# Attention and a top-2 mixture of experts in one kernel: the first expert's weights are split later and on VectorE, its early units start after one matrix, and they take two steps a tile

## The chip, the cores and the metric

The kernel runs on one core of one Trainium2 chip. The metric is device time in microseconds (us) of one execution; less is better. The runs of the kernel before took 970.3, 971.06 and 975.12 us, median 971.06. A separate execution, with the profiler, took 977.14 us; its span from the first to the last instruction is 975.3 us, and 1.8 us lie around it.

## The reference

```python
kv = np.einsum('bhsd,bhse->bhde', k, v)            # 8 batches, 8 heads, 576 rows, 64 wide
out = np.einsum('bhsd,bhde->bhse', q, kv)
rms = np.sqrt(np.mean(out * out, axis=-1, keepdims=True) + 1e-06)
x = (out / rms * g_norm)                           # as 4608 rows (tokens) of 512
...
noisy_logits = x @ w_gate + np.log1p(np.exp(x @ w_noise)) * noise
top2 = np.argpartition(-noisy_logits, 2, axis=1)[:, :2]     # 2 of 8 experts a token
...                                                # top2_w: softmax over the two
for e in range(E):
    for k in range(2):
        mask = top2[:, k] == e
        h = np.maximum(x[mask] @ w1[e], 0.0)       # 512 -> 1024
        out[mask] += top2_w[mask, k, None] * (h @ w2[e])    # 1024 -> 512
```

All inputs and the output are float32.

## The kernel before

The engines are called PE (matmul), PEld (its weight loads), DVE (VectorE), ACT (ScalarE), POOL (GpSimd) and SP (which issues DMAs). Each engine runs its own queue in order; the order of the code is the order of every queue.

**Attention.** The 4608 tokens are 36 tiles of 128. A tile's matmuls (`tile_mm`, L590) multiply q with a prepared k'v of its batch; four of the tiles lie across two batches, so there are 40 pieces. `prep` (L551 to L581) makes the next batch's k'v in steps between the pieces: PE matmuls L558, L568 and L577, with ACT copies L563, L571 and L580 between them. `advance` takes finished tiles on: ACT copies a tile out of the two PSUM buffers "big" (L598) and squares it (L605), DVE sums the squares (L607), ACT makes the root (L611, L612), POOL scales (L621, L625), DVE adds up the logits (L630), ACT issues the store of x to DRAM (L634). After a piece PE gets KW = 8 small matmuls of zeros (`keep_warm`, L124) while the tile number is under KT = 24; they compute nothing that is used.

**Gating.** After tiles 10, 18, 28 and 36 a chunk of tokens is gated (`chunk`, `gating`): the two experts of each token, the place of each token in its expert's list (`onehots` L304 to L310, `place` L318) and the gate's weight. `finish` (L325) turns expert 0's list, as far as it is known, into row numbers and gates, and `scale_gates` multiplies the gates with a constant "c" that is known when both of the expert's matrices have been scaled. These steps are generators; `pump` takes them on, several times a tile.

**Experts.** Float32 is split into two float16 halves, and three matmuls take the place of one. `weights` (L214) loads w1 and w2 of an expert (`load_w1` L206, `load_w2` L212, on SP), finds the largest value of each (L221 on DVE, four times), gets it to all partitions through PE (L232), and splits the matrix. For experts 1 to 7 ACT writes the high half with the scale (L255) and DVE the low half (L257). For expert 0 ACT scales in place (L250), copies the high half (L251), and POOL subtracts (L248). Expert 0's steps are taken on twice a tile from tile W1 = 2.

Work on an expert goes in units of token tiles. A unit gathers its rows of x (`gather`, L360), transposes them (`xpose`, L385 on PE for the first units), does the first layer (`l1`, L434, out through ACT L439 and DVE L440) and the second (`l2`, L478, out through ACT L503), and scatters its results (`scatter`, L412). The units are numbered from 0; expert 0 has units 0 to 4. Units 0 to 2 (EARLY) of two tiles each begin while attention still runs: `moe_early` waits until "c" is known and all of expert 0's weights are in, then puts the unit's `l1` and `l2` into `early`, and `fill_early`, once after each tile, takes one step: 12 matmuls of L434 or 6 of L478. Expert 1 begins with unit 5. After attention `bg` holds the next experts' background steps: `locate` makes an expert's list (L318 into M), `prepare` its weights.

Before the first scatter the output must be zero: `clear` (L402) issues 18 DMAs of 512 KB from a row of zeros. Here ACT issues them, one beside each early step once attention is over (`held`).

All DMAs of SP and ACT share eight semaphores, given out in turn, so a DMA waits for the one that had its semaphore before, and what stands behind it on its engine waits as well.

Of the kernel before, what the change touches and what calls it, by code (L numbers as in the profile page):

```python
# [14 lines left out]
AF = mybir.ActivationFunctionType  # L15
# [16 lines left out]
CHUNKS = (10, 18, 28, 36)  # L32
SL, W1 = 2, 2
KT, KV2 = 24, 0
XW, PY = 2, 6
LAG = 2
KC, KR, KQ, KX, KO = 5, 1, 4, 3, 3
GY = 3
WY = 4
YG, YX = 5, 2  # L40
KW0, KW1, KW = 100, 10, 8
# [10 lines left out]
def attention_moe(ctx: ExitStack, tc: tile.TileContext, kvm, kvr, qt, gn, wgn, noise, w1, w2, out):  # L52
# [160 lines left out]

    def weights(e, pool, lo, slack=0):  # L214
        WT[e] = w = {}
# [27 lines left out]

        def split(src, hi, lw, s):
            if lo is G:
                for c in range(5):
                    if c:
                        G.tensor_tensor(lw[:, c - 1], src[:, c - 1], hi[:, c - 1], OP.subtract)  # L248
                    if c < 4:
                        A.activation(src[:, c], src[:, c], AF.Copy, scale=s)  # L250
                        A.activation(hi[:, c], src[:, c], AF.Copy)  # L251
                    yield
                return
            for c in range(4):
                A.activation(hi[:, c], src[:, c], AF.Copy, scale=s)  # L255
                if c:
                    lo.scalar_tensor_tensor(lw[:, c - 1], src[:, c - 1], s, hi[:, c - 1], op0=OP.mult, op1=OP.subtract)  # L257
                yield
            lo.scalar_tensor_tensor(lw[:, 3], src[:, 3], s, hi[:, 3], op0=OP.mult, op1=OP.subtract)
            yield  # L260
            yield
# [9 lines left out]
        w["w1l"] = pool.tile([P, 4, FF], F16, name="w1l")  # L271
        yield from split(r1, w["w1h"], w["w1l"], sc[:, 1:2])
        for _ in range(min(slack, 3)):
            yield
        if (e, 1) not in RW:
# [12 lines left out]
        w["w2l"] = pool.tile([P, 4, FF], F16, name="w2l")  # L288
        yield from split(r2, w["w2h"], w["w2l"], sc[:, 4:5])
        for k in ("w2h", "w2l"):  # L290
# [108 lines left out]
    def clear():  # L399
        r = next(blank, None)  # L400
        if r is not None:
            zeroed.append(A.dma_start(ov[:, r:r + 2], zrow[:, None, :].to_broadcast([P, 2, DM])).ins)  # L402
            return True
# [66 lines left out]
    def l2(u):  # L470
# [18 lines left out]
        for i, t in enumerate(tiles):  # L489
            if tail:  # L490
                ps = pss[i]
            else:
                ps = ps_tile([P, DM])
                for f in range(0, 8, 2):
                    mms(ps, i, (f, f + 1))
                    if f < 6:
                        yield
            if len(outs) == 4:
                while clear():
                    pass  # L500
                scatter()
            y = moe_a.tile([P, DM], F32, name="y", bufs=4)
            A.activation(y, ps, AF.Copy, scale=LG[e][:, t:t + 1])  # L503
            outs.append((y, e, t))
            if u >= EARLY:
                scatter()
            yield
# [6 lines left out]
    def moe_early(u):  # L514
        while "c" not in WT[0]:
            yield 1
        finish(0, M0, slice(2 * u, 2 * u + 2))
        yield 1
        gather(u)
        yield YG  # L520
        while 0 not in loaded:
            yield 1
        yield from xpose(u)
        early.extend([l1(u), l2(u)])

    early = deque()
    held = [0]
    ready, loaded = {0}, set()

    with tc.tile_pool(name="p1", bufs=2) as p1, tc.tile_pool(name="ps1", bufs=1, space=PSUM) as ps1:  # L530
# [148 lines left out]
        def fill_early():  # L679
            while early:  # L680
                try:
                    next(early[0])
                    if held[0] and not clear() and held[0] > 1:
                        scatter()
# [4 lines left out]
        def first_weights():  # L689
            yield from weights(0, wts_a, G, SL)  # L690
            loaded.add(0)
# [12 lines left out]
        for b in range(B):  # L704
# [4 lines left out]
            if b + 1 < B:  # L709
                load_q(b + 1, 1)  # L710
            if b + 2 == B:
                load_w1(1)
            steps = prep(b + 1) if b + 1 < B else iter(())
            for args in per[b]:
                t = args[0]
                tile_mm(*args)
                keep_warm(KW if t < KT else KV2)
                next(steps, None)
# [14 lines left out]
            drain(steps)  # L733
        held[0] = 1
        for t in range(NT, NT + 4):
# [19 lines left out]
    def prepare(e):  # L755
        yield from weights(e, wts_b if e % 2 else wts_a, V)
        if e in ready:
# [6 lines left out]
    def locate(e):  # L764
        M = psl.tile([P, 5 * CAP], F32, name="M")
        last = None
        for q in range(5):
            oh = (yield from onehots(e, 9 * q, 9 * q + 9)) if q < 4 else None
            if q:
# [10 lines left out]
    def fill():  # L780
        hold[0] -= 1
        if bg and hold[0] <= 0:
            try:
                hold[0] = next(bg[0]) or 1
            except StopIteration:
                bg.popleft()

    bg.append(prepare(1))
    k = 0
    while side:  # L790
        pump()
        fill_early()
        k += 1
        if k % 2:
            fill()
    finish(0, M0, slice(2 * EARLY, CAP))
    gather(EARLY)
    held[0] = 2
    tot = rout.tile([P, E], F32, name="tot")
# [12 lines left out]
    V.tensor_scalar(over[:, 0:1].bitcast(I32), over[:, 1:2], float(CAP * P), None, op0=OP.is_gt)  # L812
    bg.appendleft(locate(1))
    if GB > 4:
# [13 lines left out]
    for u in range(EARLY, len(units) + 1):  # L828
        if u < len(units):
# [10 lines left out]
            if u > EARLY:  # L840
                while clear():
                    pass
                scatter()
# [103 lines left out]
```

## Time and profile before

| | |
|---|---|
| runs | 970.3, 971.06, 975.12 us |
| profiled execution | 977.14 us, span 975.3 us, mean granted clock 0.965 |
| PE busy | 916.5 us (94% of the span) |
| DVE, ACT, POOL busy | 445.7, 327.5, 387.5 us |
| moved by DMA | 143.33 MB, mean 147 GB/s |
| filler L124 | 406 matmuls, 32.9 us |

Matmuls are pipelined and their modelled ends overlap, so PE's work is best read from starts. Idle time is listed with what ended it; the idle time of an engine matters only where another one waits for it.

### The profile page before, as it was taken

The numbers are of one execution on the slowest core, as the hardware profiler recorded it, in microseconds if no ns is written. First come the engines' busy times: TensorE is split into PE (matmuls) and PEld (weight loads), VectorE is DVE, ScalarE is ACT, GpSimd is POOL, SyncE is SP. The second block draws the span as 40 slices with busy tenths as digits, with TensorE's granted clock in tenths as the row PEclk, the third lists the DMA queues.
The fourth block names the chain that finished last, engine by engine and source line by source line (L and its number), as shares of the span: only waits on it lengthen the run. The fifth ranks groups of instructions, "written<-read, shape, count | busy, mean of one in ns | idle before, by whom it ended". The sixth has DMA issues, their size and how long they took to land. (4 is left out here: it accounts for less than half of the span.)

```text
span 975.3 us, 15946 instructions
## 1 busy us (share of the span) xinstructions
PE 916.5 (94%) x6484; PEld 517.2 (53%) x6484; DVE 445.7 (46%) x936; ACT 327.5 (34%) x519; POOL 387.5 (40%) x412
## 2 busy tenths in 40 slices
PE   9976888988999999999999999999998989999995
PEld 8866775657444644464445444554443434644452
DVE  1648658554745543545353444455264447311110
ACT  1576543222522341233224332333243223332111
POOL 0456645153523542344245234414342544242122
PEclk9978799988999999999999999999999999999998
DMA  8999655952963864485357544666349735362224
GB/s 329 364 348 350 207 195 198 385 98 57 254 116 76 169 169 60 97 171 135 84 102 132 152 116 92 142 104 164 66 120 127 187 76 92 50 113 45 44 37 58
DMA packets 123534, 143.33 MB, mean 147 GB/s; under 512 B 79632, under 2 KB 79760, under 8 KB 123408
## 3 DMA queue, kind: packets, MB, share of 16 engines
q1 hardware_dynamic: 95696, 80.68, 30.2%
q0 software_dynamic: 17920, 41.95, 23.2%
q10 hardware_dynamic: 9792, 18.88, 5.1%
q8 instruction: 97, 1.59, 0.7%
q14 instruction: 29, 0.24, 0.1%
HBM read 83.02 MB, written 40.11 MB: 126 GB/s over the span
## 5 line engine op out<-in xcount | busy, mean ns | idle before, releaser
L434 PE MATMUL pp<-xT,w1h 128*128 128x512 f16 (+5 forms) x1600 | 367.8, 327 | 5.9 <-DVE oa L304 2.6
L478 PE MATMUL pp<-w2h,hT 128*128 128x512 f16 x1200 | 365.6, 381 | 5.4 <-ACT hT L439 4.1
L478 PEld LDWEIGHTS <-hT 128*128 128x128 f16 x1800 | 175.9, 98 | 214.0 <-issue 9.3
L412 POOL DMA_INDIRECT out_rows<-y,row x80 | 129.9, 1624 | 359.2 <-ACT y L503 354.5
L440 DVE SCALAR_TENSOR_TENSOR hT<-pp,hT 128x512 f16<-128x512 f32 x160 | 108.0, 688 | 353.7 <-ACT hT L439 353.6
L434 PE MATMUL pp<-xT,w1l 128*128 128x512 f16 (+5 forms) x800 | 256.8, 327 | 0.0
L478 PE MATMUL pp<-w2l,hT 128*128 128x512 f16 x600 | 228.2, 380 | 0.0
L434 PEld LDWEIGHTS <-w1h 128*128 128x128 f16 x1600 | 151.2, 100 | 112.2 <-issue 8.0
L439 ACT ACTIVATE hT<-pp 128x512 f16<-128x512 f32 x160 | 92.5, 596 | 265.7 <-PE pp L434 255.1
L503 ACT ACTIVATE y<-pp,gate 128x512 f32<-128x512 f32 x80 | 54.0, 686 | 258.6 <-PE pp L478 201.5
L360 POOL DMA_INDIRECT xg<-xs,idx x80 | 85.0, 1063 | 91.7 <-DVE la L332 43.5
L434 PEld LDWEIGHTS <-w1l 128*128 128x128 f16 x800 | 79.8, 100 | 56.5 <-issue 1.8
L368 POOL TENSOR_TENSOR xh<-xg,xh 128x512 f16<-128x512 f32 x70 | 91.4, 1380 | 35.7 <-ACT xh L367 35.6
L221 DVE TENSOR_REDUCE mx<-rw 128x1 f32<-128x1024 f32 x64 | 74.7, 1208 | 1.3 <-DMA rw<-w 1.3
L367 ACT ACTIVATE xh<-xg 128x512 f16<-128x512 f32 x70 | 41.1, 624 | 22.7 <-DMA xg<-xs,idx 18.8
L590 PE MATMUL big<-kvw,qt 64*128 64x80 f32 (+1 forms) x640 | 45.5, 287 | 2.2 <-ACT kvw L580 2.1
L304 DVE TENSOR_TENSOR oa<-jb,lnb 128x1152 bf16<-128x1152 bf16 (+2 forms) x32 | 46.3, 1448 | 0.0
L590 PEld LDWEIGHTS big<-kvw,qt 64*128 64x128 f32 (+1 forms) x640 | 39.1, 189 | 8.2 <-ACT kvw L580 2.8
L607 DVE TENSOR_REDUCE ss<-sq 128x16 f32<-128x1024 f32 x18 | 21.9, 1215 | 47.2 <-ACT sq L605 47.1
L411 POOL MEMSET tick<- 1x1 f32 x80 | 38.7, 484 | 0.0
L625 POOL TENSOR_TENSOR x<-o,ss 128x512 f32<-128x512 f32 x36 | 38.0, 1076 | 0.0
L257 DVE SCALAR_TENSOR_TENSOR w1l<-rw,sc,w1h 128x1024 f16<-128x1024 f32 x21 | 27.3, 1333 | 22.3 <-ACT w1h L255 22.3
(140 smaller groups left out, 587.7 us busy)
## 6 DMA issues: line engine op xcount, KB each, us to landing
rw<-w SPq DMA_DIRECT2D x64, 512.0 KB, 7.2
kvc<-kvm SPq DMA_DIRECT2D x32, 512.0 KB, 8.0
xs<-x ACTq DMA_DIRECT2D x18, 512.0 KB, 5.9
out_rows<-zrow ACTq DMA_DIRECT2D x18, 512.0 KB, 7.5
qt<-qt SPq DMA_DIRECT2D x8, 640.0 KB, 8.3
qt<-qt SPq DMA_DIRECT2D x8, 512.0 KB, 7.9
kvr<-kvr SPq DMA_DIRECT2D x4, 512.0 KB, 6.9
xg<-xs,idx POOLq DMA_INDIRECT x80, 3.9
```

The lines of the kernel that those rows point to most:

```text
L221: V.tensor_reduce(mx[:, c:c + 1], src[:, c], axis=AX.X, op=OP.max, apply_absolute_value=True)
L304: V.tensor_tensor(oa, jb[:, None, :].to_broadcast([P, n, P]), lnb[:, s, e:e + 1].to_broadcast([P, n, P]), OP.is_equal)
L360: G.indirect_dma_start(out=x, out_offset=None, in_=src, in_offset=bass.IndirectOffsetOnAxis(ap=LI[e][:, t:t + 1], axis=0))
L367: A.activation(x[:, 0], XG[u, t], AF.Copy)
L368: G.tensor_tensor(x[:, 1], XG[u, t], x[:, 0], OP.subtract)
L412: d = G.indirect_dma_start(out=out, out_offset=bass.IndirectOffsetOnAxis(ap=LS[e][:, t:t + 1], axis=0), in_=y, in_offset=None, compute_op= ...
L434: T.matmul(ps[:, f % ps.shape[1], 0:n], w[wn][:, c, f * P:(f + 1) * P], x[:, xo + c, 0:n], start=(c == 0 and k == 0), stop=(c == HP - 1 an ...
L439: A.activation(h[:, 0, f:f + nf, 0:n], ps, AF.Relu)
L440: V.scalar_tensor_tensor(h[:, 1, f:f + nf, 0:n], ps, 0.0, h[:, 0, f:f + nf, 0:n], op0=OP.max, op1=OP.subtract)
L478: T.matmul(ps, h[:, hk, f, i * P:(i + 1) * P], w[wn][:, f], start=(f == 0 and k == 0), stop=(f == 7 and k == 2))
L503: A.activation(y, ps, AF.Copy, scale=LG[e][:, t:t + 1])
L590: T.matmul(TL[t][r0:r0 + n, h, hp * 80:(hp + 1) * 80], q[r, hp, s0 - o:s0 - o + n], KVW[b][r, hp], start=True, stop=True, skip_group_check ...
```

## The change

- W1 goes from 2 to 7: expert 0's weights start five tiles later. KT goes from 24 to 16: no filler from tile 16 on.
- Expert 0's split is done as the other experts': one ACT instruction and one DVE instruction a quarter, and with `slack` one more step between them.
- A flag "half" is set when w1 is split. `moe_early` now finishes the list and gathers without waiting for "c"; gates that lack "c" are kept in `bare` and multiplied when the weights are done. Transposes and `l1` wait for "half" alone; `second` lets `l2` wait for all weights. YG, the steps between gather and transposes, goes from 5 to 7.
- `fill_early` is called twice a tile.
- The 18 zeroing DMAs go to SP's queue, all at the start of batch 6 (tile 27), ahead of expert 1's w1.
- After attention expert 1's `locate` comes before its `prepare` and begins while the last chunk is still being gated (its last quarter waits for that); a background step is taken at every turn instead of every other, and scatters begin after the last list is finished. XW, the steps ahead of the transposes of units 3 and 4, goes from 2 to 5.

```diff
-SL, W1 = 2, 2
-KT, KV2 = 24, 0
-XW, PY = 2, 6
+SL, W1 = 2, 7
+KT, KV2 = 16, 0
+XW, PY = 5, 6
...
-YG, YX = 5, 2
+YG, YX = 7, 2
...
-        def split(src, hi, lw, s):
-            if lo is G:
-                for c in range(5):
-                    if c:
-                        G.tensor_tensor(lw[:, c - 1], src[:, c - 1], hi[:, c - 1], OP.subtract)
-                    if c < 4:
-                        A.activation(src[:, c], src[:, c], AF.Copy, scale=s)
-                        A.activation(hi[:, c], src[:, c], AF.Copy)
-                    yield
-                return
+        def split(src, hi, lw, s, slack=0):
             for c in range(4):
                 A.activation(hi[:, c], src[:, c], AF.Copy, scale=s)
+                if slack:
+                    yield
                 if c:
-                    lo.scalar_tensor_tensor(lw[:, c - 1], src[:, c - 1], s, hi[:, c - 1], op0=OP.mult, op1=OP.subtract)
+                    V.scalar_tensor_tensor(lw[:, c - 1], src[:, c - 1], s, hi[:, c - 1], op0=OP.mult, op1=OP.subtract)
                 yield
...
-        yield from split(r1, w["w1h"], w["w1l"], sc[:, 1:2])
-        for _ in range(min(slack, 3)):
-            yield
+        yield from split(r1, w["w1h"], w["w1l"], sc[:, 1:2], slack)
+        w["half"] = True
...
-            zeroed.append(A.dma_start(ov[:, r:r + 2], zrow[:, None, :].to_broadcast([P, 2, DM])).ins)
+            zeroed.append(SP.dma_start(ov[:, r:r + 2], zrow[:, None, :].to_broadcast([P, 2, DM])).ins)
...
     def moe_early(u):
-        while "c" not in WT[0]:
-            yield 1
         finish(0, M0, slice(2 * u, 2 * u + 2))
+        if "c" not in WT.get(0, ()):
+            bare.append(slice(2 * u, 2 * u + 2))
         yield 1
         gather(u)
         yield YG
-        while 0 not in loaded:
+        while "half" not in WT.get(0, ()):
             yield 1
         yield from xpose(u)
-        early.extend([l1(u), l2(u)])
+        early.extend([l1(u), second(u)])
+
+    def second(u):
+        while 0 not in loaded:
+            yield
+        yield from l2(u)
...
+            while bare:
+                scale_gates(0, bare.pop())
             loaded.add(0)
...
             if b + 2 == B:
+                while clear():
+                    pass
                 load_w1(1)
...
                 tile_mm(*args)
+                fill_early()
                 keep_warm(KW if t < KT else KV2)
...
-        held[0] = 1
...
         for q in range(5):
+            while q == 3 and side:
+                yield 1
...
+    bg.append(locate(1))
     bg.append(prepare(1))
-    k = 0
     while side:
         pump()
         fill_early()
-        k += 1
-        if k % 2:
-            fill()
+        fill()
     finish(0, M0, slice(2 * EARLY, CAP))
     gather(EARLY)
-    held[0] = 2
+    held[0] = 1
...
-    bg.appendleft(locate(1))
```

Three places of the order show what moves. The first is ACT's queue at the split of expert 0's w1. Before, around tile 11 (`o` and `sq` are attention's copy and square, `kvw` is the k'v copy L563, `ss` the root):

```order
L605 ACTIVATE sq<-o 128x1024
L250 ACTIVATE rw<-rw,sc 128x1024
L251 ACTIVATE w1h<-rw 128x1024
L250 ACTIVATE rw<-rw,sc 128x1024
L251 ACTIVATE w1h<-rw 128x1024
L563 ACTIVATE kvw<-kvt 128x4x64
L611 ACTIVATE ss<-ss,eps 128x16
L612 ACTIVATE ss<-ss 128x16
L598 ACTIVATE o<-big 128x640
```

And now, around tile 15:

```order
L601 ACTIVATE sq<-o 128x1024
L246 ACTIVATE w1h<-rw,sc 128x1024
L559 ACTIVATE kvw<-kvt 128x4x64
L154 ACTIVATE gt_d<-gt_d 128x10
L607 ACTIVATE ss<-ss,eps 128x16
L608 ACTIVATE ss<-ss 128x16
L594 ACTIVATE o<-big 128x640
L246 ACTIVATE w1h<-rw,sc 128x1024
```

Four split instructions stood ahead of the k'v copy; now it is one, and the next comes after the next tile's copy.

The second is SP's queue from the loads of the last batches' k, v and q (`kvc`, `qt`) on. Before:

```order
L536 DMA kvc<-kvm 128x1024 x4
L548 DMA qt<-qt 128x1280 x2
L548 DMA qt<-qt 128x1024
L206 DMA rw<-w 128x1024 x4
L212 DMA rw<-w 128x2x512 x4
```

And now; the second matrix of expert 0 (`rw`, first row) has moved here, from ahead of batch 5's k and v to ahead of batch 7's:

```order
L212 DMA rw<-w 128x2x512 x4
L544 DMA qt<-qt 128x1024
L532 DMA kvc<-kvm 128x1024 x4
L544 DMA qt<-qt 128x1280 x2
L544 DMA qt<-qt 128x1024
L394 DMA out_rows<-zrow 128x2x512 x18
L206 DMA rw<-w 128x1024 x4
```

The zeroing stands between the last load of q and expert 1's w1.

The third is DVE's queue after attention, where the last chunk's lists are made (`oa`, `ob` of 128x1024 and 128x400 belong to the last chunk of expert 0, those of 128x1152 and 128x450 to `locate` of expert 1). Before, nothing of `locate` stands there, and the weights of expert 1 are being scaled (`sc`):

```order
L196 CAST vals<-gt_w 128x64
L304 TENSOR_TENSOR oa<-jb,lnb 128x1024
L307 TENSOR_TENSOR ot<-tb_101,t_115 128x80
L310 TENSOR_TENSOR ob<-ot,vals 128x400
L234 TENSOR_REDUCE al<-pp 128x1
L235 TENSOR_SCALAR al<-al 128x1
```

And now:

```order
L302 TENSOR_TENSOR ob<-ot,vals 128x450
L196 CAST vals<-gt_w 128x64
L381 TENSOR_TENSOR xT<-pp,xT 128x4x128
L296 TENSOR_TENSOR oa<-jb,lnb 128x1024
L299 TENSOR_TENSOR ot<-tb_101,t_115 128x80
L302 TENSOR_TENSOR ob<-ot,vals 128x400
L296 TENSOR_TENSOR oa<-jb,lnb 128x1152
```

Two quarters of expert 1's lists are now made before the last chunk's, between its steps, the other two follow at once, and expert 1's weights come after.

On PE the first matmul of unit 0's first layer stands after tile 25 (before: after tile 24); each tile then has two early steps instead of one, and when the last tile's matmuls are issued unit 0 is done and 24 matmuls of unit 1 stand before them, where before unit 0 had 30 of its 48 second-layer matmuls left. From the first matmul of expert 1 on, PE's order is the same.

More of the change, by code (lines that the diff above doesn't have):

```diff
@@ L212, in load_w2, with weights @@
             SP.dma_start(r[:, c].rearrange("p (f d) -> p f d", f=2), v[c])
-    def weights(e, pool, lo, slack=0):
+    def weights(e, pool, slack=0):
         WT[e] = w = {}
@@ L242, in scale @@
             yield
-        def split(src, hi, lw, s):
-            if lo is G:
-                for c in range(5):
-                    if c:
-                        G.tensor_tensor(lw[:, c - 1], src[:, c - 1], hi[:, c - 1], OP.subtract)
-                    if c < 4:
-                        A.activation(src[:, c], src[:, c], AF.Copy, scale=s)
-                        A.activation(hi[:, c], src[:, c], AF.Copy)
-                    yield
-                return
+        def split(src, hi, lw, s, slack=0):
             for c in range(4):
                 A.activation(hi[:, c], src[:, c], AF.Copy, scale=s)
+                if slack:
+                    yield
                 if c:
-                    lo.scalar_tensor_tensor(lw[:, c - 1], src[:, c - 1], s, hi[:, c - 1], op0=OP.mult, op1=OP.subtract)
+                    V.scalar_tensor_tensor(lw[:, c - 1], src[:, c - 1], s, hi[:, c - 1], op0=OP.mult, op1=OP.subtract)
                 yield
-            lo.scalar_tensor_tensor(lw[:, 3], src[:, 3], s, hi[:, 3], op0=OP.mult, op1=OP.subtract)
+            V.scalar_tensor_tensor(lw[:, 3], src[:, 3], s, hi[:, 3], op0=OP.mult, op1=OP.subtract)
             yield
@@ L288, in weights @@
         w["w2l"] = pool.tile([P, 4, FF], F16, name="w2l")
-        yield from split(r2, w["w2h"], w["w2l"], sc[:, 4:5])
+        yield from split(r2, w["w2h"], w["w2l"], sc[:, 4:5], slack)
         for k in ("w2h", "w2l"):
@@ L498, in l2 @@
             if len(outs) == 4:
-                while clear():
-                    pass
                 scatter()
@@ L520, in moe_early @@
         yield YG
-        while 0 not in loaded:
+        while "half" not in WT.get(0, ()):
             yield 1
         yield from xpose(u)
-        early.extend([l1(u), l2(u)])
+        early.extend([l1(u), second(u)])
[3 more added lines that the diff above has]
+        yield from l2(u)
     early = deque()
+    bare = []
     held = [0]
@@ L682, in fill_early @@
                     next(early[0])
-                    if held[0] and not clear() and held[0] > 1:
+                    if held[0]:
                         scatter()
@@ L689, in first_weights @@
         def first_weights():
-            yield from weights(0, wts_a, G, SL)
+            yield from weights(0, wts_a, SL)
+            while bare:
+                scale_gates(0, bare.pop())
             loaded.add(0)
@@ L755, in prepare @@
     def prepare(e):
-        yield from weights(e, wts_b if e % 2 else wts_a, V)
+        yield from weights(e, wts_b if e % 2 else wts_a)
         if e in ready:
@@ L840, in attention_moe @@
             if u > EARLY:
-                while clear():
-                    pass
                 scatter()
```

## The prediction

> **What bounds the kernel now.** I cut the span at the starts of attention tiles 0, 14 and 24, at the end of the last attention tile's matmuls, and at the first matmul of expert 1, and asked for busy time in these windows. The columns are the window, its length, then busy us (instructions) of PE, PEld, DVE, ACT and POOL, the granted clock, the DMA share and GB/s.
>
> ```profile
> core 0: us, PE busy (x) PEld busy (x) DVE busy (x) ACT busy (x) POOL busy (x), PEclk, DMA share, GB/s
> 0.00:19.20 19.20, 17.44 (x293) 16.51 (x293) 2.57 (x16) 2.48 (x4) 1.00 (x8) 1.00 0.86 325
> 19.20:70.20 51.00, 43.52 (x769) 38.02 (x768) 24.73 (x46) 30.97 (x52) 24.88 (x24) 0.87 0.94 351
> 70.20:113.20 43.00, 33.10 (x508) 29.01 (x506) 29.91 (x132) 25.29 (x45) 28.68 (x33) 0.80 0.80 295
> 113.20:154.30 41.10, 36.52 (x471) 29.13 (x469) 27.21 (x104) 21.67 (x44) 18.51 (x25) 0.96 0.52 180
> 154.30:254.60 100.30, 87.70 (x656) 60.79 (x655) 59.37 (x159) 27.32 (x45) 38.81 (x47) 0.91 0.67 199
> 254.60:960.00 705.40, 694.83 (x3788) 342.40 (x3786) 301.88 (x481) 218.46 (x328) 271.73 (x273) 1.00 0.54 111
> ```
>
> From 254.6 us on PE is busy for 694.83 of 705.40 us at full clock, and the change leaves that order of instructions as it is: this part is carried over unchanged. All that can move lies before. I call the four windows from 19.2 to 254.6 **first** (tiles 0 to 13), **second** (tiles 14 to 23), **third** (tiles 24 to 35, with early expert work between them) and **bridge** (the rest of expert 0). In none of them is PE full: 7.5, 9.9, 4.6 and 12.6 us are idle, and the clock is under 1.
>
> Next I asked who PE waited for, first from 50 to 113 us, then in the bridge. The columns are the waiting and the awaited instruction, us in total, times, longest.
>
> ```profile
> PE kvt L568 <- ACT kvw L563: 5.9, 2, 3.9
> PE kvt L577 <- ACT kvT L571: 4.7, 2, 3.4
> PE big L590 <- ACT kvw L580: 2.1, 2, 1.6
> ```
>
> ```profile
> PE pp L385 <- DMA xg<-xs,idx: 5.9, 2, 3.6
> PE M L318 <- DVE ob L310: 3.3, 1, 3.3
> PE pp L232 <- DVE dg L228: 1.6, 1, 1.6
> PE RM L318 <- DVE ob L310: 1.5, 1, 1.5
> ```
>
> So 12.7 us of the 17.4 us idle in the first two windows are waits for ACT in the k'v preparation of the next batch. ACT's timeline shows why ACT was late: it was in the split of expert 0's first matrix.
>
> ```profile
> 52.18 1.06 ACT L251 ACTIVATE w1h<-rw 128x1024 f16<-128x1024 f32 x1
> 53.14 1.13 ACT L250 ACTIVATE rw<-rw,sc 128x1024 f32<-128x1024 f32 x1
> 54.30 1.06 ACT L251 ACTIVATE w1h<-rw 128x1024 f16<-128x1024 f32 x1
> 55.27 0.36 ACT L563 ACTIVATE kvw<-kvt 128x256 f32<-128x256 f32 x1
> ```
>
> The reader sees two pairs back to back, and L563, for which PE stands still, behind them. PE's timeline at the same place shows the second cost, a slow clock after the gap (start, length, line, idle in brackets):
>
> ```profile
> 55.69 1.06 PE L568 MATMUL kvt<-ident,kvw 128*64 128x128 f32 x4 [3.94 <-ACT kvw L563]
> 56.72 2.00 PE L590 MATMUL big<-kvw,qt 64*128 64x80 f32 x16
> ...
> 71.75 1.12 PE L590 MATMUL big<-kvw,qt 64*128 64x80 f32 x16
> 72.81 0.62 PE L124 MATMUL RM<-zrow 128*128 128x128 f16 x8
> ```
>
> The same 16 matmuls of a tile take 2.00 us at 56.72 and 1.12 at 71.75.
>
> **The split (first and second window).** These are the groups of the split before, and the DVE instruction that the other experts use for the low half, which expert 0 now uses too:
>
> ```profile
> L250 ACT ACTIVATE rw<-rw,sc 128x1024 f32<-128x1024 f32 x8 | 9.1, 1138 | 4.1 <-DVE sc L241 2.2 <-DVE sc L238 1.9
> L251 ACT ACTIVATE w1h<-rw 128x1024 f16<-128x1024 f32 x4 | 4.2, 1056 | 0.1
> L251 ACT ACTIVATE w2h<-rw 128x1024 f16<-128x1024 f32 x4 | 4.2, 1057 | 0.1
> L248 POOL TENSOR_TENSOR w1l<-rw,w1h 128x1024 f16<-128x1024 f32 x4 | 8.5, 2128 | 4.3 <-ACT w1h L251 4.3
> L257 DVE SCALAR_TENSOR_TENSOR w1l<-rw,sc,w1h 128x1024 f16<-128x1024 f32 x21 | 27.3, 1333 | 22.3 <-ACT w1h L255 22.3
> ```
>
> ACT loses eight 1.06 us passes (8.4 us). POOL loses twice 8.5 us and was not waited for by PE, so that is worth nothing by itself. DVE gains 8 x 1.333 = 10.7 us, half in the second window, half in the third. The order puts one split instruction of ACT between attention's, two pieces of the old block never together, so the 3.9 us wait and its twin for the second matrix lose their cause; what is late next is DVE's chain or a load.
>
> First window: 7.5 us idle at most, and nothing at least, because the load of w1 now starts at tile 7, behind the loads of the next batch on SP's queue, at 351 GB/s, and DVE's first reduction of it can wait there, with the sums of squares queued behind it and ACT waiting for those. I take 5 us, about the block from 52 us on and the slow clock after it.
>
> Second window: DVE was busy 29.91 us and gets 4 x 1.333 = 5.3 more, so it can't be under 35.2 us; the data, 295 GB/s x 43.0 us = 12.7 MB, at the first window's 351 GB/s needs 36.1. The gain is thus at most 6.9 us. Nine of the filler groups (0.62 us each, 5.6 us) go as well, but they lie inside that bound and are no term of their own. DVE may also wait for w2, whose load now stands behind batch 6's on SP. At least it is nothing; I take 5.
>
> **The third window and the two steps a tile.** Early unit 0 starts its first layer after tile 25 (before: 24), but does it two steps a tile, and its second layer too. By the last tile 30 more matmuls of L478 and 24 more of L434 are issued. Their price, from PE's rows: 18 of L478 from 185.21 to 189.09 (0.216 each) and 24 of L434 to 191.71 (0.109):
>
> ```profile
> 185.21 0.38 PE L478 MATMUL pp<-w2h,hT 128*128 128x512 f16 x1
> ...
> 189.09 0.38 PE L434 MATMUL pp<-xT,w1h 128*128 128x256 f16 x2
> ...
> 191.71 0.37 PE L318 MATMUL RM<-ob,oa 128*128 128x50 bf16 x8
> ```
>
> That is 6.5 + 2.6 = 9.1 us, paid in the third window and saved in the bridge: it moves work and gains nothing by itself. It would gain where it filled an idle PE, at most the 4.6 us idle there; but DVE goes from 27.21 to 32.5 us with w2's low half, and w2's ACT passes now stand here, so it may also lose as much. I take nought.
>
> **The zeroing.** Eighteen DMAs of 512 KB move from ACT's queue after the last tile to SP's, ahead of w1 of expert 1, at the start of batch 6. In the bridge they held ACT up:
>
> ```profile
> 169.86 7.59 ACTq L402 DMA_DIRECT2D out_rows<-zrow  x2
> 177.50 0.60 ACT L439 ACTIVATE hT<-pp 128x512 f16<-128x512 f32 x1 [7.07 <-DMA rw<-w]
> ```
>
> Now they are 18 x 0.524 = 9.4 MB, 27 us at 351 GB/s, in a window that used 180 GB/s of it. What is queued behind them on SP is w1 of expert 1, before at 121.70, first needed now after unit 3 has begun, late in the bridge: hidden.
>
> ```profile
> 121.70 2.42 SPq L206 DMA_DIRECT2D rw<-w  x4
> ```
>
> **The bridge.** Lists of expert 1 (L318 M) now come before its weights, and the pieces that PE waited 3.3 us for stand between early steps. Between the placing of the last tokens and unit 3's transposes PE has 24 + 36 early matmuls, 2.6 + 7.8 = 10.4 us, where before it reached them early and waited 3.6 us for the rows; unit 2's 2.3 us go likewise. That is 9.2 us at most. Against it: with 9.1 us less early work to hide the last tokens' gating, and unit 2's results now waiting behind the first scatters, some of the waits come back; the 1.6 us for L228 stays. At least nothing; I take 5.
>
> **Sum.** 5 + 5 + 0 + 5 = 15 us. The profiled execution took 977.1 us (span 975.3, 1.8 around it), so it would take 962.1. It lies 6.1 us above the median of the runs, 971.06, and 15 off the median gives **956**. With the ends together: 7.5 + 6.9 + 9.2 = 23.6 gives 947; 2 + 2 + 1 = 5, what I would still call this case, gives 966.
>
> **Rivals.** A measurement of this kernel tells a change from none at about 0.5%, 4.9 us.
>
> *The front is held anyway* (0.17). DMA is at 0.94 in the first window, and DVE stands near its floor in the second; if loads and DVE replace ACT as the wait, tile 24 starts at 113 again and only the bridge gains: 971 - 0 to 5, so 966 to 971. For it: DVE's 5.3 us more. Against it: the waits on record name ACT.
>
> *The clock falls without filler* (0.11). From tile 16 on PE has real work for half a tile's time. The matmuls after the 3.94 us gap ran at 2.00 for 1.12, and a gap of 1.47 was enough too:
>
> ```profile
> 77.48 0.64 PE L577 MATMUL kvt<-gw,kvT 64*64 64x16 f32 x16
> ...
> 135.87 0.63 PE L385 MATMUL pp<-ident,xg 128*128 128x128 f32 x4 [1.47 <-DVE ss L613]
> 136.43 1.01 PE L577 MATMUL kvt<-gw,kvT 64*64 64x16 f32 x16
> ```
>
> (L577: 1.01 for 0.64.) Nine groups without filler at 0.88 us more are 7.9 us: 956 + 8 = 964. [...]
>
> *Slower: zeroing chokes the third window* (0.10). The eight hardware DMA semaphores are taken in turn, and ACT's stores of x wait for zeroing DMAs that had the semaphore before, as L439 did for 7.07 us; unit 1's gather runs in the same stretch, and PE, in order, stands at its transposes before the next tile:
>
> ```profile
> 130.25 0.99 POOL L360 DMA_INDIRECT xg<-xs,idx  x1 [4.11 <-DVE la L332]
> ```
>
> Transposes followed that gather after 5.6 us (135.87). With three such waits, 3 x 7.07 = 21 us, less the 10 us of the first two windows: 982. It decides from the point where a zeroing DMA lands later than three tiles after its issue (3 x 41.1 / 12 = 10 us); before, they landed in 7.5:
>
> ```profile
> out_rows<-zrow ACTq DMA_DIRECT2D x18, 512.0 KB, 7.5
> ```
>
> *All of it comes* (0.10): the bounds above and some of the third window's idle, 944 to 947.
>
> **How the numbers follow.** The forecast has 0.52. Faster by over 0.5%: 0.52, the last rival's 0.10, 0.08 of the clock's 0.11 and 0.05 of the held front's 0.17, together 0.75. Within 0.5%: 0.12 of the held front and 0.03 of the clock, 0.15. Slower: 0.10. The range reaches from 944 to 973: it takes in the forecast's 947 to 966, the held front and the clock, and leaves out the slower case and the extreme of the best.
>
> **What would show it.** Right: no wait of over 2 us of PE for L563's and L571's counterparts; tile 24 at about 103 us; the last tile ending at 150 to 156 in spite of 9 us more work in it; expert 1's first matmul at about 240. Wrong: tile 24 still at 113 with PE or ACT waiting for DVE or a load; ACT's stores of x waiting for out_rows between tiles 28 and 35; the second window's clock under 0.80; or waits of 10 us and more in the bridge, so that what the front gains is given back.

## The result, and the profile after

The changed kernel took 960.98 us (median of 10 runs, 955.41 to 964.66), the kernel before in the same sitting 971.94 us (965.55 to 977.01): ratio 0.9896, 95% interval 0.9871 to 0.992. That is faster by 11.0 us, 1.0%; 956 had been forecast, with 944 to 973 as range. The profiled execution took 961.43 us, 15.7 less than that of before.

Cut at the same five places (tile 0, tile 14, tile 24, the end of the last tile's matmuls, expert 1's first matmul), the changed kernel's windows read:

```profile
core 0: us, PE busy (x) PEld busy (x) DVE busy (x) ACT busy (x) POOL busy (x), PEclk, DMA share, GB/s
0.00:19.36 19.36, 17.60 (x291) 16.67 (x292) 2.57 (x16) 2.48 (x4) 1.00 (x8) 1.00 0.85 326
19.36:63.84 44.48, 41.17 (x769) 36.37 (x767) 20.36 (x46) 22.95 (x44) 16.39 (x20) 0.92 0.95 360
63.84:100.19 36.35, 27.13 (x435) 24.04 (x431) 34.21 (x129) 20.38 (x40) 18.51 (x24) 0.81 1.02 378
100.19:152.28 52.09, 46.83 (x528) 34.59 (x527) 35.88 (x125) 28.27 (x52) 25.11 (x35) 0.97 0.92 339
152.28:240.78 88.50, 76.38 (x600) 52.68 (x600) 57.13 (x150) 24.46 (x42) 35.11 (x42) 0.92 0.49 119
240.78:959.60 718.82, 696.89 (x3803) 343.57 (x3801) 301.29 (x481) 219.97 (x331) 275.38 (x277) 0.99 0.54 110
```

Against before: first window 51.0 to 44.5 us, second 43.0 to 36.4, third 41.1 to 52.1, bridge 100.3 to 88.5, the rest 720.7 to 718.8. In the second window DVE is now busy for 34.21 of 36.35 us and the DMA share is 1.02: DVE has taken ACT's place, and no wait of PE or DVE there names a load. PE's waits there (the columns are as before: us in total, times, longest):

```profile
PE big L586 <- ACT kvw L576: 3.5, 2, 2.8
PE RM L310 <- DVE ob L302: 3.3, 1, 3.3
PE kvt L573 <- ACT kvT L567: 1.7, 1, 1.7
```

No wait is left for the copy that was L563 (now L559), and for L571's counterpart L567 at most 1.7 us; before, the longest were 3.9 and 3.4. A new wait for DVE, at the lists, has come. The longest for L580's counterpart L576 has grown from 1.6 to 2.8 us; just before that copy ACT itself had waited 2.30 us for DVE, in the gating (at 89.47 us).

In the bridge there is a new wait as well. This is the longest row of PE's waits in the bridge:

```profile
PE pp L426 <- ACT xT L380: 6.1, 2, 5.1
```

ACT's timeline shows what its transposed rows (L380) stood behind:

```profile
189.43 0.60 ACT L431 ACTIVATE hT<-pp 128x512 f16<-128x512 f32 x1 [2.23 <-PE pp L426]
203.43 0.69 ACT L493 ACTIVATE y<-pp,gate 128x512 f32<-128x512 f32 x1 [13.40 <-DMA out_rows<-y,row]
204.01 0.59 ACT L380 ACTIVATE xT<-pp 128x512 f16<-128x512 f32 x1
205.81 0.69 ACT L493 ACTIVATE y<-pp,gate 128x512 f32<-128x512 f32 x1 [1.21 <-DMA out_rows<-y,row]
```

There are four buffers for results (`y`). The fifth waits 13.4 us until the first scatter has read one out; the first scatter is issued at 198.51, behind unit 3's gathers, though the fourth result had been ready at 172.3:

```profile
193.44 0.99 POOL L352 DMA_INDIRECT xg<-xs,idx  x1 [17.96 <-DVE m L327]
198.51 1.62 POOL L404 DMA_INDIRECT out_rows<-y,row  x1 [0.22 <-issue]
```

### The profile page after: what moved, and what is told of

It is laid out like the page before. It is cut to its first block, busy times and chain, and to the rows that moved or that the text cites. A ratio compares the mean times of both kernels' runs of the same rounds, so it can differ in the third digit from the quotient of the medians.

```text
span 959.6 us, 15796 instructions
## 1 busy us (share of the span) xinstructions
PE 906.0 (94%) x6412; PEld 507.9 (53%) x6412; DVE 451.4 (47%) x944; ACT 318.5 (33%) x511; POOL 371.5 (39%) x404
## 5 line engine op out<-in xcount | busy, mean ns | idle before, releaser
L426 PE MATMUL pp<-xT,w1h 128*128 128x512 f16 (+5 forms) x1600 | 366.6, 326 | 14.1 <-ACT xT L380 6.1
L470 PE MATMUL pp<-w2h,hT 128*128 128x512 f16 x1200 | 365.1, 380 | 4.2 <-ACT hT L431 4.2
L470 PEld LDWEIGHTS <-hT 128*128 128x128 f16 x1800 | 175.2, 98 | 210.9 <-issue 4.7
L426 PE MATMUL pp<-xT,w1l 128*128 128x512 f16 (+5 forms) x800 | 255.4, 326 | 0.0
L470 PE MATMUL pp<-w2l,hT 128*128 128x512 f16 x600 | 227.6, 379 | 0.0
L426 PEld LDWEIGHTS <-w1h 128*128 128x128 f16 x1600 | 149.8, 99 | 119.2 <-issue 9.6
L426 PEld LDWEIGHTS <-w1l 128*128 128x128 f16 x800 | 79.1, 99 | 58.4 <-issue 3.7
L586 PE MATMUL big<-kvw,qt 64*128 64x80 f32 (+1 forms) x640 | 46.4, 289 | 3.7 <-ACT kvw L576 3.7
L586 PEld LDWEIGHTS big<-kvw,qt 64*128 64x128 f32 (+1 forms) x640 | 39.8, 192 | 10.5 <-ACT kvw L576 4.6
L250 DVE SCALAR_TENSOR_TENSOR w1l<-rw,sc,w1h 128x1024 f16<-128x1024 f32 x24 | 31.1, 1327 | 23.5 <-ACT w1h L246 23.5
L621 POOL TENSOR_TENSOR x<-o,ss 128x512 f32<-128x512 f32 x36 | 40.0, 1132 | 0.0
```

The source lines that it names most:

```text
L426: T.matmul(ps[:, f % ps.shape[1], 0:n], w[wn][:, c, f * P:(f + 1) * P], x[:, xo + c, 0:n], start=(c == 0 and k == 0), stop=(c == HP - 1 an ...
L470: T.matmul(ps, h[:, hk, f, i * P:(i + 1) * P], w[wn][:, f], start=(f == 0 and k == 0), stop=(f == 7 and k == 2))
L586: T.matmul(TL[t][r0:r0 + n, h, hp * 80:(hp + 1) * 80], q[r, hp, s0 - o:s0 - o + n], KVW[b][r, hp], start=True, stop=True, skip_group_check ...
```

## The experiments

The **theory** after this reading: the split's form and its later start free the front; the second step only moves work; the zeroing, in the third window, loads the DMA engines; the bridge gains by the early lists and loses by the queue behind the first scatters. The **rivals** are in the expectations. Each kernel has one edit to the changed kernel where nothing else is said; times are medians, ratios are to the kernel before on the same chip (its medians 970.71 to 971.75). Line numbers are those of the changed kernel (L951 and L952 are the old split's two passes; L586 is a tile's matmuls, L426 and L470 are the two layers, L377 the transposes, L380 and L381 their copies, L310 the matmuls of the lists and L302 what DVE makes for them). The same instructions in the same order took 42.9 to 45.7 us in the first window and 718.0 to 721.2 in the last part, so a difference of under 3 us in one window tells nothing by itself. In the bridge the changed kernel's order took 85.4 us in one of the runs below (the filler until tile 23) and 88.5 in its own; in the third window the order with one step took 48.3 and 43.4.

**Scatters allowed from the end of attention on.**

```diff
-            drain(steps)
+            drain(steps); held[0] = int(b == B - 1)
```

> The changed kernel with one edit: results of the early units may be scattered from the end of attention on, not only after the last gather of unit 3. In the changed kernel PE waited 5.05 us at 207.04 us for ACT's transposed rows, which stood behind a result (y) that waited 13.4 us for the first scatters to free its buffer. Theory (the new wait is that queue on ACT, and the change put it there): four scatters now run in the 18 us in which POOL had nothing to do, ACT's wait shrinks below 2 us, and 3 to 5 us go: 956 to 958. Rival (PE would wait for the gathered rows or for DVE anyway): the wait changes its name and less than 1.5 us goes: 959.5 to 961.

It took 952.94 us, ratio 0.9814 (0.9783 to 0.9846), 8.0 less than the changed kernel. POOL's timeline, and the bridge:

```profile
151.13 1.63 POOL L404 DMA_INDIRECT out_rows<-y,row  x1 [0.16 <-issue]
...
168.49 1.57 POOL L404 DMA_INDIRECT out_rows<-y,row  x1 [0.40 <-ACT xT L380]
```

```profile
147.90:230.34 82.44, 73.19 (x600) 51.96 (x601) 58.12 (x150) 25.02 (x42) 36.72 (x43) 0.98 0.52 126
```

Four scatters now run before 170 us, ACT's wait of 13.4 us is gone, PE's for L380 is 1.1 us in place of 6.1, and the bridge is 82.4 us long in place of 88.5. The wait was the queue on ACT, and the theory holds. Its price is less sure than the 8.0: 4.4 of the 8.8 us between the two profiled executions lie ahead of tile 35's end, where the edit changes nothing, and in the bridge PE's idle time falls by 2.9 us, from 12.1 to 9.2.

**The old split, at the new place.** Expert 0's quarters go through two ACT passes and POOL, two quarters to a tile, as before.

```diff
-        yield from split(r1, w["w1h"], w["w1l"], sc[:, 1:2], slack)
+        yield from split(r1, w["w1h"], w["w1l"], sc[:, 1:2], slack) if e else old_split(nc, r1, w["w1h"], w["w1l"], sc[:, 1:2])
...
-        yield from split(r2, w["w2h"], w["w2l"], sc[:, 4:5], slack)
+        yield from split(r2, w["w2h"], w["w2l"], sc[:, 4:5], slack) if e else old_split(nc, r2, w["w2h"], w["w2l"], sc[:, 4:5])
```

> The changed kernel with the split of expert 0's two matrices done as before the change: two ACT passes a quarter, low half on POOL, quarters two to a tile; everything else stays as changed. Theory (the front was held by ACT in the split): the waits of PE for the k'v copy, 3 to 4 us each, come back, first and second window get 8 to 12 us longer, and it takes 969 to 973. Rival (the front gained because the first matrix is loaded and split later and PE has early work in the idle places, not because of the split's form): the front gets at most 3 us longer, 961 to 964.

(`old_split` is the loop of the kernel before, put at the end of the file.) It took 978.03 us, ratio 1.0049 (1.0024 to 1.0075): 17 us more than the changed kernel, and more than the kernel before. The first window stays at 45.1 us, since at tile 7 the split no longer lies in it. The loss is in the next two:

```profile
63.61:104.56 40.95, 31.74 (x437) 28.30 (x433) 34.12 (x117) 24.01 (x42) 27.71 (x33) 0.71 0.83 322
104.56:168.17 63.61, 55.15 (x550) 39.71 (x549) 33.17 (x113) 32.24 (x58) 28.26 (x31) 0.87 0.75 278
```

The second is 4.6 us longer and the third 11.5. In the third, ACT's passes for the second matrix stand ahead of unit 0's transposed rows, and PE's first layer stands behind those:

```profile
107.00 1.14 ACT L951 ACTIVATE rw<-rw,sc 128x1024 f32<-128x1024 f32 x1
108.17 1.06 ACT L952 ACTIVATE w2h<-rw 128x1024 f16<-128x1024 f32 x1
109.13 1.13 ACT L951 ACTIVATE rw<-rw,sc 128x1024 f32<-128x1024 f32 x1
110.30 1.06 ACT L952 ACTIVATE w2h<-rw 128x1024 f16<-128x1024 f32 x1
111.26 0.58 ACT L380 ACTIVATE xT<-pp 128x512 f16<-128x512 f32 x1
```

```profile
111.89 0.37 PE L426 MATMUL pp<-xT,w1h 128*128 128x256 f16 x1 [4.60 <-ACT xT L380]
```

That wait of 4.6 us is a part of the 11.5: PE is idle for 8.5 us of the third window in place of 5.3, does 22 matmuls more in it, and has a clock of 0.87 in place of 0.97. The form matters, then, and most at the new place. My theory had the loss in the first and second window; 11.5 us of it came in the third.

**The new split alone, in the kernel before.** One word: expert 0's low halves go to `V` in place of `G`.

```diff
-            yield from weights(0, wts_a, G, SL)
+            yield from weights(0, wts_a, V, SL)
```

> The kernel before with one part of the change alone: expert 0's two matrices are split in the form that the other experts use (one ACT pass a quarter, low half on DVE); the weights still begin at tile 2. Theory (the form frees ACT in both windows): the first window goes from 51.0 to 46 us, as with the new form at tile 2 in the changed kernel (46.1), the second gains 0 to 3 us of 43.0, since DVE's reductions of the second matrix now stand ahead of the lists there, and it takes 963 to 967. Rival (the form is worth nothing without the later start): 970 to 973.

It took 963.53 us, ratio 0.9927 (0.99 to 0.9953): 7.2 us of the 11.0 come from this part by itself. Its windows, first to third:

```profile
18.24:66.96 48.72, 44.01 (x768) 39.08 (x766) 28.19 (x73) 26.77 (x48) 18.26 (x20) 0.86 0.97 368
66.96:102.27 35.31, 30.02 (x509) 26.59 (x505) 32.48 (x113) 20.80 (x40) 19.25 (x25) 0.90 0.92 349
102.27:139.71 37.44, 33.81 (x466) 27.49 (x465) 29.05 (x105) 21.76 (x45) 21.51 (x30) 1.00 0.60 218
```

The time is as expected, its places are not: the first window gains 2.3 us, within the spread, and the second 7.7. The third is 3.7 us shorter than that of before at a clock of 1.00 against 0.96.

**The weights of expert 0 begun at tile 2 again** (the split in its new form).

```diff
-SL, W1 = 2, 7
+SL, W1 = 2, 2
```

> The changed kernel with the weights of expert 0 begun at tile 2, as before the change, and not at tile 7; the split keeps its new form. Theory (the first window became shorter because its loads and split went out of it, not because of the split's form; the old form, tried at tile 7, left that window at 45.1 us): the first window gets 3 to 6 us longer, 47.5 to 50.5, the second 2 to 4 shorter, and it takes 961 to 965. Rival (the form alone frees the first window): the first window stays within 1.5 us of 44.5, and it takes 957 to 961.

It took 970.22 us, ratio 0.9963 (0.9931 to 0.9995), 9 us more than the changed kernel. The first window is 46.1 us, near the spread; the second and the third take 42.5 and 54.8. PE waits 10.5 us for the lists, and DVE's timeline shows why:

```profile
PE RM L310 <- DVE ob L302: 10.5, 1, 10.5
```

```profile
75.69 1.22 DVE L221 TENSOR_REDUCE mx<-rw 128x1 f32<-128x1024 f32 x1 [4.96 <-DMA rw<-w]
...
81.12 2.34 DVE L221 TENSOR_REDUCE mx<-rw 128x1 f32<-128x1024 f32 x2
83.38 2.17 DVE L296 TENSOR_TENSOR oa<-jb,lnb 128x1280 bf16<-128x1280 bf16 x1
...
86.77 0.66 DVE L302 TENSOR_TENSOR ob<-ot,vals 128x500 bf16<-128x500 bf16 x1
```

The reductions of the second matrix stand on DVE ahead of the first chunk's lists, and the first of them waits 5 us for its load. Both theories fall: the later start is worth nothing measurable in the first window, and keeps a load off DVE's queue in the second. The start at tile 2 alone does not do this: with the new split alone (above), also begun at tile 2, the second window took 35.3 us and DVE waited for no load there. SP's queue differs. The second matrix (L212) went ahead of four loads of k and v there, and stands behind them here; first the split alone (in its numbers L536 is the load of k and v, L532 here), then this run:

```profile
57.43 4.05 SPq L212 DMA_DIRECT2D rw<-w  x4
62.82 7.20 SPq L536 DMA_DIRECT2D kvc<-kvm  x4
```

```profile
57.49 7.09 SPq L532 DMA_DIRECT2D kvc<-kvm  x4
65.19 3.84 SPq L212 DMA_DIRECT2D rw<-w  x4
```

The changed kernel's split takes more steps (`slack`), and the load is issued after it. That the extra steps are what moved it behind those loads is read from the code; no run has the start at tile 2 without them in the changed kernel.

**The filler until tile 23.**

```diff
-KT, KV2 = 16, 0
+KT, KV2 = 24, 0
```

> The changed kernel with the filler matmuls for PE's clock on until tile 23, as before the change, and not 15. Theory (the second window is held by DVE, and nine groups of 0.62 us lie in PE's idle time): within 2 us of the changed kernel, 959 to 963. First rival (without filler the clock falls, and attention's matmuls there run slower): the granted clock of the second window rises from 0.83 to 0.9 and over and 4 to 8 us go, 953 to 957. Second rival (filler costs PE what it takes): 5 us more, 966.

It took 963.76 us, 0.8 above the theory's range, ratio 0.9922 (0.9891 to 0.9953): its interval overlaps that of the changed kernel. The second window:

```profile
63.96:101.22 37.26, 31.34 (x506) 27.83 (x502) 33.91 (x125) 20.36 (x40) 18.52 (x24) 0.86 0.99 371
```

The clock is 0.86 against 0.81 and the window no shorter, so the first rival is out. PE is idle for 5.9 us of it in place of 9.2: the filler lies in idle time. That DVE holds the window, busy for 33.9 of 37.3 us, fits this and is not shown by itself.

**One early step a tile.**

```diff
                 tile_mm(*args)
-                fill_early()
```

> The changed kernel with one early step a tile and not two. Theory (the second step moves 9 us of PE work from the bridge into the third window and gains nothing by itself): the third window gets 7 to 10 us shorter, the bridge as much longer, and it stays within 2 us, 959 to 963. Rival (the second step puts work where PE stands idle, which the bridge can't hide): the third window gets only 3 us shorter, and it takes 965 to 968.

It took 954.46 us, ratio 0.9816 (0.9781 to 0.9851), 6.5 less than the changed kernel; neither the theory nor the rival had expected that. The third window and the bridge:

```profile
100.14:148.42 48.28, 40.80 (x468) 31.83 (x467) 36.36 (x125) 26.52 (x49) 23.85 (x31) 0.82 0.98 364
148.42:234.00 85.58, 81.83 (x660) 56.03 (x660) 56.35 (x150) 26.90 (x45) 35.37 (x44) 1.00 0.49 119
```

The third window is 3.8 us shorter, and the bridge, with 60 matmuls more in it (660 to 600), is no longer for them; the 2.9 us that it is shorter lie within what one order takes (85.4 to 88.5). Over all the runs here that take expert 0's weights as the changed kernel does, the third window took 49.9 to 52.4 us with two steps and 42.8 to 48.3 with one. The work that the second step takes out of the bridge had covered waits there: PE was idle in it for 12.1 us with two steps and 3.8 with one.

**Both, one step and early scatters.**

```diff
-                fill_early()
...
-            drain(steps)
+            drain(steps); held[0] = int(b == B - 1)
```

> The changed kernel with one early step a tile and with scatters allowed from the end of attention on: the two edits that took 6.5 and 8 us off it one by one. If they take away different waits, both come: 946 to 948. Rival (with one step a tile the bridge has 9 us more early work, which already covers the wait that the earlier scatters take away; its waits were down to 3.7 us): 952 to 955.

It took 953.39 us, ratio 0.9812 (0.9777 to 0.9848), like each alone: the rival holds. Both edits take away the same waits in the bridge. With the scatters early, the second step does cost nothing (952.94 with two, 953.39 with one).

**Expert 1's lists later, as before.**

```diff
-    bg.append(locate(1))
     bg.append(prepare(1))
...
+    bg.appendleft(locate(1))
```

(Also, as before, the background goes on only at every second step of that loop.)

> The changed kernel with expert 1's lists made after the last tokens' routing and behind the start of its weights, as before the change. Theory (the early lists take away waits of PE in the bridge, 5 us): the bridge gets 4 to 6 us longer, 965 to 967. Rival (the bridge is held by the queue on ACT behind the first scatters, which this leaves as it is, or by PE's own work): within 2 us of the changed kernel, 959 to 963.

It took 967.18 us, ratio 0.9951 (0.993 to 0.9972), 6.2 more: the theory holds for the time. The bridge is 91.7 us long, 3.2 more than the changed kernel's where 4 to 6 were expected, and the wait of before is back with its 3.3 us:

```profile
PE M L310 <- DVE ob L302: 3.3, 1, 3.3
```

The run undoes the early lists, their place ahead of the weights and the pace of the background together, so it doesn't tell which of the three is worth what.

**The zeroing behind attention, on SP's queue.** It is issued after expert 1's first matrix and the last tile.

```diff
-                while clear():
-                    pass
                 load_w1(1)
...
-    drain(w0)
+    drain(w0), list(iter(clear, None))
```

> The changed kernel with the zeroing of the output moved from ahead of expert 1's first matrix, at the start of the last batch but one, to behind the last tile of attention; it stays on SP's queue. Theory (the zeroing is not hidden: in the changed kernel the DMA engines are busy 1.02 to 1.05 of the time from 115 to 140 us, and the third window, of 52.1 us, is held by them): the third window gets 4 to 6 us shorter, the bridge, where the DMA share was 0.49, stays within 2 us, and it takes 955 to 958. First rival (hidden, as the prediction had it): 959 to 963. Second rival (the zeroing is now in the way of the gathers and the scatters of the bridge): 964 to 968.

It took 959.46 us, ratio 0.9888 (0.9846 to 0.993): no difference from the changed kernel. In the third window the DMA share goes from 0.92 to 0.71, and its length from 52.1 to 50.7:

```profile
99.74:150.41 50.67, 46.66 (x528) 34.27 (x527) 36.90 (x125) 28.27 (x52) 24.70 (x35) 0.97 0.71 256
```

The theory falls and the prediction's account, hidden, stands: PE itself is busy for 46.7 of the 50.7 us.

**The zeroing behind attention, on ACT's queue**, one or more at each early step, as before.

```diff
-            zeroed.append(SP.dma_start(ov[:, r:r + 2], zrow[:, None, :].to_broadcast([P, 2, DM])).ins)
+            zeroed.append(A.dma_start(ov[:, r:r + 2], zrow[:, None, :].to_broadcast([P, 2, DM])).ins)
```

> The changed kernel with the zeroing of the output back on ACT's queue and behind attention, one or more at each early step, as before the change; everything else stays as changed. Placed there on SP's queue it took 959.46 us, no more than where the change put it, so the place is not the matter; this asks for the queue. Theory (on ACT's queue a zeroing DMA that waits keeps ACT from its next result, before the change for 7.07 us, but PE had other work meanwhile): within 3 us of the changed kernel, 958 to 964. Rival (ACT's queue was what the bridge waited for, and taking the zeroing off it is a gain of its own): the bridge gets 4 to 8 us longer, 965 to 969.

The rest of the edit, not printed, puts back the calls of `clear` and the values of `held` of the kernel before. It took 967.59 us, ratio 0.9986 (0.9958 to 1.0014): 6.6 more than the changed kernel, and the rival holds. The bridge is 94.8 us long. ACT's timeline:

```profile
166.59 10.17 ACTq L394 DMA_DIRECT2D out_rows<-zrow  x4
176.81 0.69 ACT L493 ACTIVATE y<-pp,gate 128x512 f32<-128x512 f32 x1 [9.55 <-DMA out_rows<-zrow]
...
178.03 0.60 ACT L380 ACTIVATE xT<-pp 128x512 f16<-128x512 f32 x1 [0.54 <-issue]
```

Four issues take ACT 10.2 us; a result and the transposed rows of unit 2 stand behind them, and PE's waits for L380 come to 12.2 us in place of 6.1. The first of the two has grown to 7.4 us; the second, behind the scatters, is as long as in the changed kernel (4.8 and 5.1).

**The same with one step a tile.**

```diff
                 tile_mm(*args)
-                fill_early()
...
-            zeroed.append(SP.dma_start(ov[:, r:r + 2], zrow[:, None, :].to_broadcast([P, 2, DM])).ins)
+            zeroed.append(A.dma_start(ov[:, r:r + 2], zrow[:, None, :].to_broadcast([P, 2, DM])).ins)
```

> The changed kernel with one early step a tile and with the zeroing back on ACT's queue behind attention. With two steps that queue cost 6.6 us (967.59 against 960.98); with one step and the zeroing as changed it took 954.46. Theory (the second step takes away the PE work that hid what ACT's queue loses): with one step 24 + 30 more matmuls cover it again, the bridge gets at most 3 us longer than 85.6, and it takes 954 to 958. Rival (ACT's queue holds the bridge whatever PE still has to do): 960 to 963.

It took 957.71 us, ratio 0.9861 (0.9821 to 0.9902), 3.3 more than one step with the zeroing on SP, half of the 6.6 with two, and the intervals overlap:

```profile
143.43:232.49 89.06, 82.51 (x660) 55.79 (x661) 57.94 (x153) 27.10 (x45) 36.70 (x45) 1.00 0.75 220
```

The rest of the edit is as above. The bridge is 3.5 us longer than with one step alone, 0.5 over the bound that I had set. This fits the theory, that PE's work covers ACT's queue in part, but six runs do not tell 3.3 us from none, nor from the 6.6.

**Combined:** one step, the zeroing behind attention on SP, four scatters ahead of unit 3's gathers.

```diff
-                fill_early()
...
-                while clear():
-                    pass
...
-    drain(w0)
+    drain(w0), list(iter(clear, None))
...
-    finish(0, M0, slice(2 * EARLY, CAP))
+    scatter(), finish(0, M0, slice(2 * EARLY, CAP))
```

> A version meant to beat both: the changed kernel with one early step a tile, the zeroing behind the last tile on SP's queue, and the four results that are ready scattered ahead of the last gather of unit 3. With one early step the third window had 36.0 to 40.8 us of PE work in 43.4 to 48.3 us and the DMA engines at 0.98 and 0.99 of it. Theory (there, with less of PE's work, the zeroing does hold it): the third window gets to about 41, and it takes 949 to 952. Rival (PE's own waits hold it, for the gating and for DVE, 7 us): 952 to 955, as each edit alone.

It took 953.89 us, ratio 0.983 (0.9792 to 0.9868): the rival holds. The third window took 47.0 us where the theory had 41. The best version remains either edit alone, at 953 to 954.5 us, some 1.8% below the kernel before; these runs do not tell the two apart.

## Why the prediction was right, and where not

**First window, 5 us forecast: 6.5.** The block of ACT passes is gone from it, and no wait for the copy is left. Which part does it, the runs don't tell: the window took 46.1 us with the new form at tile 2, 45.1 with the old form at tile 7, and 48.7 with the new form alone in the kernel before. The fear that the load at tile 7 would wait on SP came true in small: SP waited 9.4 us for a store of x before it could issue the third quarter, DVE's reduction of that quarter waited 1.92 us, and PE 1.90 us for the largest value that hangs on it.

**Second window, 5 us with a bound of 6.9: 6.7.** It went to the bound: DVE's floor had been put at 35.2 and that of the data at 36.1, and the window took 36.35. The nearness of the second number is luck, since the data came at 378 GB/s and not at 351, and PE's idle time stayed (9.2 us after 9.9). What I did not see is that the new split, in the form that the changed kernel gives it, needs the later start: with the old start a reduction waits for its load ahead of the lists on DVE, and 9 us are lost. In the kernel before, the new split with the old start lost nothing here (35.3 us).

**Third window and two steps, nought forecast: a loss of 6.5.** This is the step that failed. "Paid in the third window and saved in the bridge" was half right: it is paid (the window took 52.1 us, and 42.8 to 48.3 in the executions with one step), but the bridge gave nothing back for it, since without that work PE stands in waits there, idle for 12.1 us in place of 3.8. The rest of the window's growth from 41.1 us is there with one step too; DVE is busy for 36 us of it in place of 27, and what that costs was not tried by itself. With the scatters early the step does net to nought. I had named the cause in the bridge ("unit 2's results now waiting behind the first scatters"), and priced it inside a term of 5 instead of asking what the moved work had covered.

**Zeroing, hidden: right for the place, wrong for the queue.** In the third window it costs nothing (959.46 us with it elsewhere), and it landed in 9.7 us, just under the 10 us that the slower rival needed; ACT's stores of x did not wait for it (the five issues between 111 and 152 us took 0.38 to 0.47 us each). But taking it off ACT's queue was given no price; PE's waits in the bridge before name no ACT instruction. With two steps a tile that queue would have cost 6.6 us; the 3.3 with one are not clear of noise.

**Bridge, 5 us forecast.** The early lists and the faster background are worth 6.2 together, the new wait behind the scatters costs up to 8.0. Expert 1's first matmul came at 240.78, where about 240 had been forecast; that agreement is partly luck: an unpriced gain (ACT's queue) and an unpriced loss (the second step) cancel.

**The sum.** Against the profiled execution 15 us had been forecast and 15.7 came; against the medians it is 11.0. The profiled execution of before lay 5.2 us above the median of 971.94 us, that of after 0.5 above its own, so the sum was worked out on an execution that lay above the median and then taken off the median. That is most of the distance from 956 to 961. Where those 5 us lay stays open: the third window, where the new split alone ran 3.7 us faster at a higher clock, is one candidate.

**The rivals.** The front was not held: tile 24 starts at 100.19 us. The clock did not decide: more filler gains nothing, and without filler from tile 16 on the second window took 36.2 to 36.7 us in four runs whose clock there was 0.72, and 36.3 to 36.4 in three at 0.81. Undone one by one the parts come to 17 + 9 + 6 + 7 - 6.5 = 32.5 us, three times the gain; they cover one another, and none is worth a fixed price.

What holds four versions at 953 to 954.5 us was not found.

## What to carry to other kernels

Before work is moved out of a stage, ask which waits it covers there: moved work that "nets to nought" costs whatever stood behind it (here 6.5 us by the medians). On ACT, which took its instructions in order, a result that waited 13.4 us for a buffer, or DMAs that waited for their turn (four issues, 10.2 us, with the zeroing on its queue), held up what was queued behind them, and the cure (here scatters issued some 40 us earlier, 8.0 us by the medians) was worth nearly as much as the change itself, 11.0. A sum made on one profiled execution is to be set against that execution, and the distance of that execution from the median is an error of the forecast.

## What the runs showed of the hardware

The same PE instructions after nearly the same gaps ran at different clocks in two executions. With one step a tile:

```profile
126.40 0.63 PE L377 MATMUL pp<-ident,xg 128*128 128x128 f32 x4 [3.29 <-DVE gate L315]
...
132.12 0.58 PE L426 MATMUL pp<-xT,w1h 128*128 128x256 f16 x2 [2.69 <-DVE xT L381]
134.77 2.00 PE L586 MATMUL big<-kvw,qt 64*128 64x80 f32 x16
...
144.85 1.12 PE L586 MATMUL big<-kvw,qt 64*128 64x80 f32 x16
```

And with one step and early scatters:

```profile
126.05 0.63 PE L377 MATMUL pp<-ident,xg 128*128 128x128 f32 x4 [3.32 <-DVE gate L315]
...
131.60 0.58 PE L426 MATMUL pp<-xT,w1h 128*128 128x256 f16 x2 [2.69 <-DVE xT L381]
134.25 1.12 PE L586 MATMUL big<-kvw,qt 64*128 64x80 f32 x16
```

And in the changed kernel, where half a tile's matmuls take 0.77 us at full clock (at 31.31 us, granted 1.00):

```profile
55.32 0.80 PE L232 MATMUL pp<-dg,onef 128*128 128x128 f32 x2 [1.90 <-DVE dg L228]
56.04 1.33 PE L586 MATMUL big<-kvw,qt 64*64 64x80 f32 x16
```

In the first two the gap of 2.69 us is followed by the same slow first layer: 0.58 us for two matmuls, where two took 0.38 at 118.25 us in the one and at 117.99 in the other, as in the changed kernel at full clock (at 108.91, granted 1.00 from 108 to 116 us). Then the clock is full again from 134.25 us on in the second (granted 1.00 from 135 to 145), and only from 144.85 on in the first (granted 0.50 from 130 to 140 and 0.53 from 140 to 145): a tile's matmuls take 2.00 us in the one and 1.12 in the other, and the third windows are 48.3 and 43.4 us long. What sets the moment at which the clock comes back was not shown. In the changed kernel the clock was at half (granted 0.50 from 55.2 to 57.4 us) after a gap of 1.90 us, and half a tile's matmuls took 1.33 us for 0.77.
